# Linear attention with a channel mix on one core: the q transposes of batches 4 to 7 moved from TensorE to the DMA crossbar

## The chip, the cores and the metric

The kernel runs on one core of one Trainium2 chip. The metric is the device time of one execution in microseconds (us). Three timed runs of the kernel before gave 208.45, 209.91 and 210.52 us; the median, 209.91 us, is the time before. A core has five instruction streams that run beside each other: TensorE (PE; its weight loads are shown as PEld), VectorE (DVE), ScalarE (ACT), GpSimd (POOL) and SyncE (SP). Each works through its own list in order, and an instruction that waits for a semaphore holds back everything behind it in its list. Sixteen DMA engines move data for all of them.

## The reference

Two layers one after the other, for 8 batches, 8 heads, 576 positions and 64 numbers a head:

```
kv  = einsum('bhsd,bhse->bhde', k, v)
o   = einsum('bhsd,bhde->bhse', q, kv)
x   = o / sqrt(mean(o*o, axis=-1) + 1e-6) * g_norm        # to (batch, seq, 512)
xk  = mu_k * x + (1 - mu_k) * x_prev                      # x_prev: x one position earlier
xr  = mu_r * x + (1 - mu_r) * x_prev
out = sigmoid(xr @ w_r) * (relu(xk @ w_k)**2 @ w_v)       # w_k 512x1024, w_v 1024x512, w_r 512x512
```

## The kernel before

**Two stages.** `attention(b)` works on one batch, in two halves z of four heads each. `mix(g)` works on a group of 512 positions; there are nine groups, 0 to 8, and a group needs one or two batches (group 8 the last 512 positions, that is batch 7 alone).

**A plan of named pieces, one list.** `attention` and `mix` compute nothing at once: each `add(name, engines, function, ...)` registers a piece of work under a name. `ORDER`, a text of some 740 words at the head of the file, then says in which order the pieces are emitted, and a suffix `@A` or `@D` says whether a movable piece goes to ACT or to DVE. Since an engine works in order, `ORDER` sets the order on all five engines. The names, for batch b, half z, section i of the positions, group g:

- `ld.q b`, `ld.k b`, `ld.v b`: loads from HBM that turn float32 into bfloat16, issued by POOL (L251). Batches 0 and 1 are loaded by halves, the others whole. Each of k, v and q has three buffers.
- `q b.z` (L294): 36 TensorE transposes of 64x64 per half, into PSUM; `qc` copies the result to SBUF as `qT`.
- `kv b` (L286): k times v, 72 matmuls; `kc` copies the 128x256 result to SBUF.
- `u b.z i` (L301): q times kv, four matmuls for each section of 288 positions; `uc` copies to SBUF (`uT`), `sq` squares.
- `ss b`, `rs b`, `sp b.z`: the sum of squares of all heads (L409), the reciprocal root on ACT (L306, tile `rsc`, one buffer), and four DMAs per half, issued by SP, that spread it over the partitions (L455, tile `rs`). Batches 0 and 1 do without the spread.
- `mul`, `wr`, `d`, `mk`/`mr`, `xk`/`xr`: the normalised x and the two blends, on DVE and ACT (L423, L172/L174, L318, L178/L180, L331).
- `k g.f` (L542), `relu`, `ksq`; `r g.c` (L564), `sig`; `v g.c` (L584), `out`, `st`: the channel mix. `k`, `r` and `v` pieces are four matmuls of 512 columns with 128x128 weights. `out` multiplies on DVE, and `st` issues two DMAs to HBM (L493), on SP; only the last group also uses ACT for them.
- `z:512`: a matmul on zeros (L482), 34 of them, all in the first 20 us.

**PSUM** is split into four tiles of 128x2x512 float32. Two of them form a ring `at`, for everything in the attention, and two a ring `mm`, for the mix: a piece takes the next tile of its ring and waits until the reader of that tile's last content is done.

**SP's list** before is only `sp` and `st`: nothing in it waits for a load from HBM.

Of the kernel before, what the change touches and what calls it, by code (L numbers as in the profile page):

```python
# [25 lines left out]
mr0.1w@D mk0.1w@D ss1.0 xr0.0w ss1.1 ksq0.11 rs1.0 r0.3 xr0.1a rs1.1 q1.1 r0.0 qc1.1@D ld.k6.01 xr0.1w mul1.0 u1.11
sig0.1 u1.10 r0.1 uc1.11@D sq1.10@A v0.1.0 sq1.11@D sig0.0 xk0.1w ld.q4.01 uc1.10@D ss1.2 v0.1.1 wr1.0@D d1.0 ss1.3
v0.0.0 mk1.0@D rs1.2 xk1.0 v0.0.1 ld.v4.01 rs1.3 q2.0 mul1.1 q2.1 qc2.0@A v0.3.0 wr1.1@D d1.1 v0.3.1 out0.0 mk1.1@A
v0.2.0 st0.1 qc2.1@A xk1.1 v0.2.1 mr1.1@D k1.2 out0.1 k1.3 mr1.0@D kv2 relu1.1 k1.0 kc2@D ld.k4.01 xr1.0 ld.q5.01
u2.10 u2.01 uc2.10@D k1.1 uc2.01@A sq2.01@A sq2.10@D k1.6 relu1.0 u2.11 u2.00 uc2.11@A k1.7 uc2.00@D sq2.11@D k1.4  # L30
sq2.00@A xr1.1 relu1.3 k1.5 ksq1.3 ss2 kv3 ksq1.1 rs2 q3.0 ld.k5.01 sp2.0 r1.0 kc3@A relu1.2 qc3.0@D r1.1 ksq1.0
u3.01 q3.1 uc3.01@D sp2.1 r1.2 ld.q6.01 sq3.01@D ld.v5.01 r1.3 sig1.0 qc3.1@D ld.v6.01 ksq1.2 u3.00 u3.10 v1.0.0
uc3.00@D uc3.10@A st0.0 sq3.10@A sq3.00@D v1.0.1 sig1.1 mul2.0 u3.11 q4.1 wr2.0@D d2.0 v1.1.0 mk2.0@A v1.1.1 mul2.1
v1.3.0 qc4.1@A out1.0 v1.2.0 wr2.1@A xk2.0 uc3.11@A st1.0 v1.2.1 sq3.11@A d2.1 v1.3.1 st0.3 mk2.1@D xk2.1 ss3 kv4
out1.1 q4.0 k2.2 ld.q7.01 qc4.0@D rs3 ld.v7.01 k2.3 kc4@D sp3.0 mr2.1@D u4.11 u4.00 uc4.11@D k2.4 uc4.00@A relu2.1
sq4.11@D k2.5 sq4.00@D sp3.1 mr2.0@D u4.01 relu2.2 u4.10 uc4.01@D k2.0 sq4.10@A sq4.01@D k2.1 ksq2.1 uc4.10@A st1.1
xr2.0 ss4 relu2.0 q5.1 xr2.1 k2.6 ksq2.0 k2.7 mul3.0 qc5.1@D r2.0 relu2.3 r2.1 wr3.0@A ksq2.3 rs4 r2.2 ksq2.2 sp4.0
d3.0 r2.3 sig2.0 mk3.0@D q6.1 mul3.1 kv5 sig2.1 q5.0 qc6.1@D st1.3 v2.3.0 kc5@A qc5.0@D v2.1.0 st0.2 wr3.1@D d3.1
u5.11 u5.01 sp4.1 uc5.11@A v2.2.0 mk3.1@D uc5.01@A xk3.1 v2.3.1 mr3.1@D v2.2.1 sq5.01@D st1.2 sq5.11@D v2.0.0 xk3.0
out2.1 u5.10 kv6 uc5.10@A q6.0 ld.k7.01 mul4.0 v2.0.1 st2.2 qc6.0@A mr3.0@D v2.1.1 kc6@A sq5.10@D st2.3 xr3.1 k3.2  # L40
out2.0 u6.10 u5.00 k3.3 uc5.00@A mul4.1 st2.0 k3.4 xr3.0 relu3.1 wr4.1@D k3.5 d4.1 uc6.10@A r3.0 mr4.1@D relu3.2
sq5.00@D r3.1 sq6.10@D wr4.0@D ksq3.1 u6.01 sig3.0 ss5 uc6.01@D k3.0 d4.0 k3.1 sq6.01@D mk4.1@D rs5 kv7 mr4.0@D
relu3.0 q7.0 sp5.1 xr4.0 u6.00 k3.6 kc7@A ksq3.2 qc7.0@A k3.7 mk4.0@D ksq3.0 r3.2 relu3.3 sp5.0 uc6.00@D r3.3
sq6.00@D xk4.0 u6.11 q7.1 uc6.11@D v3.1.0 st2.1 ksq3.3 v3.0.0 sig3.1 mul5.1 v3.1.1 qc7.1@A sq6.11@D xk4.1 ss6 xr4.1
v3.0.1 r4.0 out3.0 r4.1 rs6 st3.0 u7.10 u7.11 sq7.10@A v3.2.0 uc7.11@A st3.1 uc7.10@D v3.3.0 sq7.11@D wr5.1@D sp6.0
u7.00 mul5.0 u7.01 v3.2.1 sig4.0 d5.1 v3.3.1 uc7.00@A wr5.0@A k4.6 sq7.00@A out3.1 sq7.01@A k4.7 uc7.01@A mk5.1@D
st3.2 ss7 d5.0 relu4.3 k4.2 sp6.1 mk5.0@D mr5.1@A k4.3 xk5.0 k4.4 ksq4.3 relu4.1 xr5.1 k4.5 xk5.1 k4.0 relu4.2
mul6.0 k4.1 mr5.0@D wr6.0@A d6.0 r4.2 relu4.0 r4.3 ksq4.0 k5.2 ksq4.1 sig4.1 mul6.1 k5.3 ksq4.2 v4.1.0 mr6.0@D rs7
xr5.0 v4.1.1 relu5.1 sp7.1 v4.0.0 wr6.1@A ksq5.1 v4.0.1 r5.0 out4.0 sp7.0 r5.1 mk6.0@D v4.3.0 d6.1 v4.2.0 mr6.1@D
# [25 lines left out]
class Plan:  # L75
# [8 lines left out]
    def emit(self, order, zeros):  # L84
        for word in order.split():
            if word.startswith("z:"):
                zeros(int(word[2:]))
                continue
            name, _, eng = word.partition("@")
            p = self.pieces[name]  # L90
            eng = eng or p.on
            assert len(eng) == 1 and eng in p.on and not p.done, word
            assert all(d.done for d in p.deps + p.also.get(eng, [])), word
            p.fn(eng)
            p.done = True
        assert all(p.done for p in self.pieces.values())
# [3 lines left out]
def kernel(  # L100
# [30 lines left out]
    CB = 2  # L131

# [9 lines left out]
        "kv": (2, (128, 2, NZ * HD), BF16),  # L142
# [11 lines left out]
        "mm": (2, (128, 2, 512), FP32),  # L154
        "at": (2, (128, 2, 512), FP32),
# [4 lines left out]
    def get(buf, dtype=None):  # L160
        if buf.t is None:
            n, shape, dt = BUFS[buf.tag]
            pool = psum if buf.tag in ("mm", "at") else sb
            buf.t = pool.tile(list(shape), dt, tag=buf.tag, name=buf.tag, bufs=n)
        return buf.t
# [73 lines left out]
    ps9 = Buf("at")  # L239
# [57 lines left out]
    def u_tiles(ps, kv, qT, z, c0, c1):  # L297
        for e in range(2):
            for y in range(2):
                rs_ = slice(64 * y, 64 * y + 64)  # L300
                nc.tensor.matmul(ps[64 * e:64 * e + 64, y, 0:c1 - c0], kv[rs_, e, HD * z:HD * z + HD],  # L301
                                 qT[rs_, e, c0:c1], start=True, stop=True)

# [40 lines left out]
    def section(b, z, i, name, qdep, kvc, kv, qT, uT, sq, rs):  # L344

        c0, c1 = PARTS[i] if b == 0 else (HS * i, HS * i + HS)
        w, cs = c1 - c0, slice(c0, c1)
        us = Buf("at")
        p_u = add("u" + name, "T", lambda _: u_tiles(get(us), kv.t, qT.t, z, c0, c1), deps=[qdep, kvc], bufs=[us, qT, kv])
# [12 lines left out]
    def attention(b):  # L362
# [7 lines left out]
        def kv_piece(name, ps, c, zs):  # L370
# [3 lines left out]
            return m, add("kc" + name, "DA", lambda eng: copy(eng, get(kv)[:, :, ks], ps.t[:, :, c + ks.start:c + ks.stop]),  # L374
                          deps=[m], bufs=[ps, kv])
# [9 lines left out]
        if b == 0:  # L385
            for z in range(NZ):
                _, kc = kv_piece(f"{b}.{z}", Buf("at"), 0, [z])
                kvcs.append(kc)
                for i, (c0, c1) in enumerate(PARTS):
                    qd[(z, i)] = q_piece(f"{b}.{z}{i}", z, Buf("at"), range(c0 // NP, c1 // NP), None)[1]  # L390
        else:
            ps0 = Buf("at")
            m, kc = kv_piece(f"{b}", ps0 if b > 2 else Buf("at"), KC, list(range(NZ)))
            kvcs = [kc, kc]
            for z in range(NZ):
# [257 lines left out]
```

## Time and profile before

| | |
|---|---|
| timed runs | 208.45, 209.91, 210.52 us |
| the profiled execution, its own time | 208.55 us |
| its span, first to last instruction | 206.6 us |
| VectorE, ScalarE, GpSimd busy | 137.8, 118.6, 26.4 us |
| bytes read from HBM / written | 33.56 MB / 9.44 MB |
| granted TensorE clock | 1.000 |

The span is 1.95 us shorter than the execution's own time; what lies around it is not in the profile. The costliest groups on TensorE and the groups that the change touches, in the profile's order of columns (line, engine, operation, output<-input, array tile, shape, count | busy us, mean ns of one | idle time ahead of them):

```profile
L584 PE MATMUL mm<-w_v,sqk 128*128 128x512 bf16 x272 | 62.6, 379 | 0.0
L542 PE MATMUL mm<-xk,w_k 128*128 128x512 bf16 x224 | 51.9, 379 | 0.0
L564 PE MATMUL mm<-w_r,xr 128*128 128x512 bf16 x144 | 34.1, 379 | 0.7 <-DVE w_r L180 0.7
L482 PE MATMUL mm<-zero 128*128 128x512 bf16 x34 | 10.9, 452 | 1.2 <-DVE zero L209 1.2
L294 PE MATMUL at<-ident,q 64*64 64x64 bf16 x576 | 8.0, 195 | 2.0 <-DMA q<-in_q_dram 1.2 <-ACT rs L306 0.4 <-POOL ident L224 0.4
L301 PE MATMUL at<-qT,kv 64*64 64x288 bf16 x112 | 6.7, 296 | 1.0 <-DVE qT L174 0.6 <-DVE kv L174 0.4
L286 PE MATMUL at<-v,k 64*64 64x64 bf16 x576 | 6.4, 194 | 3.4 <-ACT sig L574 1.4 <-DMA k<-in_k_dram 1.2 <-DMA v<-in_v_dram 0.7
```

The mean of one matmul is its time in the pipeline; matmuls overlap, so the time that a group takes of TensorE is its busy time. Busy time by stretches of ten us (columns: the stretch, its length, then the busy time and the count of instructions of PE, PEld, DVE, ACT and POOL, the granted clock, the DMA engines' busy share, GB/s):

```profile
20.00:30.00 10.00, 7.71 (x137) 6.39 (x138) 9.40 (x30) 8.38 (x16) 4.41 (x6) 1.00 1.22 206
50.00:60.00 10.00, 8.80 (x193) 4.30 (x192) 6.89 (x12) 6.40 (x9) 2.96 (x4) 1.00 1.20 217
80.00:90.00 10.00, 8.58 (x184) 4.30 (x183) 7.94 (x17) 5.63 (x8) 0.00 (x0) 1.00 1.19 240
100.00:110.00 10.00, 10.00 (x200) 4.85 (x196) 9.93 (x21) 9.74 (x11) 0.00 (x0) 1.00 0.35 83
150.00:160.00 10.00, 10.00 (x48) 4.56 (x47) 3.85 (x5) 3.91 (x4) 0.00 (x0) 1.00 0.23 52
```

A DMA share above 1 means that packets of several queues overlapped on an engine. It is at 1.2 while loads run and falls after 100 us.

### The profile page before, as it was taken

How to read it: one execution, taken by the hardware profiler on the slowest of the kernel's cores; microseconds unless marked ns; L12 is line 12 of the kernel's file. 1: busy time of each engine (PE TensorE's matmuls, PEld its weight loads, DVE VectorE, ACT ScalarE, POOL GpSimd, SP SyncE). 2: the span in 40 equal slices, each digit the busy share in tenths (PEclk: the TensorE clock that was granted, in tenths of full speed). 3: DMA queues.
4: the chain of work that ended last, by engine and by line, in shares of the span. 5: the costliest groups of instructions: out<-in, count | busy, mean ns of one | idle time of the engine just before them, and what ended most of it. 6: DMA issues, size and time to landing. Idle time of an engine off the chain costs nothing.

```text
span 206.6 us, 5133 instructions
## 1 busy us (share of the span) xinstructions
PE 193.2 (94%) x2172; PEld 95.7 (46%) x2172; DVE 137.8 (67%) x273; ACT 118.6 (57%) x151; POOL 26.4 (13%) x40
## 2 busy tenths in 40 slices
PE   7797979999799799799999999999999999999992
PEld 2344844544344444354443585444444444444441
DVE  1059988886585999698997798788733623421332
ACT  2279789867577395636896987716725032531310
POOL 7752532202140400000000000000000000000000
PEclk9999999999999999999999999999999999999999
DMA  4999999999999999999433650346004242604155
GB/s 75 162 207 205 206 208 205 208 216 221 210 238 236 231 252 242 223 264 268 116 91 77 149 122 0 71 94 156 0 0 102 62 93 61 143 0 102 24 133 153
DMA packets 25211, 30.10 MB, mean 146 GB/s; under 512 B 2524, under 2 KB 20708, under 8 KB 25188
## 3 DMA queue, kind: packets, MB, share of 16 engines
q0 software_dynamic: 15408, 16.78, 48.3%
q1 hardware_dynamic: 9380, 12.46, 24.0%
q10 hardware_dynamic: 400, 0.52, 0.7%
q8 instruction: 17, 0.28, 0.5%
q14 instruction: 6, 0.05, 0.1%
HBM read 33.56 MB, written 9.44 MB: 208 GB/s over the span
## 4 chain that ended last, share of the span: by engine, by line
PE 68%; DMA 20%; SPq 3%; ACT 2%; POOL 2%; issue 2%; DVE 1%; ACTq 0%; DVEq 0%; POOLq 0%
PE mm L584 26%; PE mm L542 24%; PE mm L564 12%; DMA w_r<-in_moe_w_r_dram 7%; DMA rs<-rsc 5%; DMA k<-in_k_dram 4%; DMA out_dram<-out 3%; SPq L455 2%; PE at L584 2%; PE at L301 2%; PE at L286 1%; PE at L294 1%; SPq L493 1%; POOL q L251 1%; ACT rsc L306 1%
## 5 line engine op out<-in xcount | busy, mean ns | idle before, releaser
L584 PE MATMUL mm<-w_v,sqk 128*128 128x512 bf16 x272 | 62.6, 379 | 0.0
L542 PE MATMUL mm<-xk,w_k 128*128 128x512 bf16 (+1 forms) x288 | 59.2, 356 | 0.0
L503 ACT ACTIVATE relu<-mm 128x1024 bf16<-128x1024 f32 x36 | 36.8, 1022 | 25.8 <-PE mm L542 23.4
L584 PEld LDWEIGHTS <-sqk 128*128 128x128 bf16 x296 | 28.2, 98 | 32.2 <-issue 1.4
L542 PEld LDWEIGHTS <-w_k 128*128 128x128 bf16 x288 | 27.2, 98 | 26.9 <-issue 1.6
L564 PE MATMUL mm<-w_r,xr 128*128 128x512 bf16 x144 | 34.1, 379 | 0.7 <-DVE w_r L180 0.7
L552 DVE TENSOR_TENSOR sqk<-relu 128x1024 bf16<-128x1024 bf16 x32 | 21.6, 687 | 16.4 <-ACT relu L503 16.4
L597 DVE TENSOR_TENSOR out<-mm,sig 128x1024 f32<-128x1024 f32 x16 | 19.6, 1222 | 18.6 <-PE mm L584 18.6
L574 ACT ACTIVATE sig<-mm 128x1024 bf16<-128x1024 f32 x18 | 18.3, 1024 | 22.5 <-PE mm L564 22.5
L564 PEld LDWEIGHTS <-xr 128*128 128x128 bf16 x144 | 13.7, 98 | 16.6 <-issue 1.0
L180 DVE TENSOR_SCALAR md<-d,cols 128x576 bf16<-128x576 bf16 (+2 forms) x62 | 18.2, 344 | 0.3
L172 ACT CAST uT<-at 128x576 bf16<-128x576 f32 (+1 forms) x18 | 11.4, 645 | 11.4 <-PE at L301 11.3
L423 DVE TENSOR_TENSOR xT<-uT,rs 128x1152 bf16<-128x1152 bf16 (+2 forms) x18 | 12.4, 686 | 4.8 <-DMA rs<-rsc 3.0
L188 ACT ACT_TABLE_LOAD x12 | 15.4, 1283 | 0.2
L174 DVE CAST uT<-at 128x576 bf16<-128x576 f32 (+1 forms) x14 | 10.4, 742 | 7.0 <-PE at L301 5.5
L318 DVE TENSOR_TENSOR d<-xT 128x1152 bf16<-128x1152 bf16 (+2 forms) x20 | 12.7, 634 | 0.8 <-ACT xT L172 0.5
L331 DVE TENSOR_TENSOR xk<-md,xT 128x1152 bf16<-128x1152 bf16 (+2 forms) x20 | 12.7, 633 | 0.6 <-ACT md L178 0.4
L331 DVE TENSOR_TENSOR xr<-md,xT 128x1152 bf16<-128x1152 bf16 (+2 forms) x20 | 12.5, 631 | 0.0
L482 PE MATMUL mm<-zero 128*128 128x512 bf16 x34 | 10.9, 452 | 1.2 <-DVE zero L209 1.2
L172 ACT COPY qT<-at 128x1152 bf16<-128x1152 bf16 (+2 forms) x8 | 8.0, 995 | 6.0 <-PE at L294 6.0
L178 ACT ACTIVATE md<-d,cols 128x256 bf16<-128x256 bf16 (+2 forms) x18 | 9.9, 600 | 1.8 <-DVE d L318 1.8
L174 DVE COPY qT<-at 128x1152 bf16<-128x1152 bf16 (+2 forms) x10 | 6.9, 693 | 4.7 <-ACT kv L172 4.2
(54 smaller groups left out, 139.3 us busy)
## 6 DMA issues: line engine op xcount, KB each, us to landing
out_dram<-out SPq DMA_DIRECT2D x67, 128.0 KB, 2.5
q<-in_q_dram POOLq DMA_DIRECT2D x6, 576.0 KB, 23.0
v<-in_v_dram POOLq DMA_DIRECT2D x6, 576.0 KB, 25.7
k<-in_k_dram POOLq DMA_DIRECT2D x6, 576.0 KB, 22.5
rs<-rsc SPq DMA_DIRECT2D x48, 72.0 KB, 5.0
q<-in_q_dram POOLq DMA_DIRECT2D x4, 288.0 KB, 9.7
k<-in_k_dram POOLq DMA_DIRECT2D x4, 288.0 KB, 11.4
v<-in_v_dram POOLq DMA_DIRECT2D x4, 288.0 KB, 11.0
```

Source lines behind the costliest of these rows:

```text
L172: nc.scalar.copy(out=dst, in_=src)
L174: nc.vector.tensor_copy(out=dst, in_=src)
L180: nc.vector.tensor_scalar(out=dst, in0=src, scalar1=col, scalar2=None, op0=ALU.mult)
L188: nc.scalar.preload_act_table_set(name)
L331: nc.vector.tensor_tensor(out=dst[:, 2 * z:2 * z + 2, r0:r0 + w], in0=md.t[:, :, cs], in1=xT[:, :, prev], op=ALU.add)
L503: nc.scalar.activation(out=get(rt), in_=ps.t, func=AF.Relu)
L542: nc.tensor.matmul(get(ps)[:, fc % 2, a0:a1], w_k_sb[:, cc, 128 * fc:128 * fc + 128], xk[:, cc, x0:x0 + a1 - a0], start=(cc == 0), stop=(c ...
L552: nc.vector.tensor_mul(out=get(sqk)[:, 2 * f2:2 * f2 + 2, :], in0=rt.t, in1=rt.t)
L564: nc.tensor.matmul(get(ps)[:, ci % 2, :], xr[:, cc, n0:n0 + 128], w_r_sb[:, cc, :], start=(cc == 0), stop=(cc == NHP - 1))
L574: nc.scalar.activation(out=get(sg), in_=ps.t, func=AF.Sigmoid)
L584: nc.tensor.matmul(get(ps)[:, bank, cs], sqk.t[:, fc, 128 * ci:128 * ci + 128], w_v_sb[:, fc, cs], start=(fc == 0), stop=(fc == NFC - 1))
L597: dv = add(f"out{g}.{c2}", "D", lambda _, ps=ps, sg=sg, ot=ot: nc.vector.tensor_mul(out=get(ot), in0=ps.t, in1=sg.t), deps=ms + [sg_done], ...
```

## The change

Four things change together.

1. **q of batches 4 to 7 (`XB = 4`) is transposed by DMA.** Instead of 36 TensorE transposes and a copy, a piece `xq b.z` issues one `dma_start_transpose` from SBUF to SBUF on SP's list. It turns the nine 128x128 blocks of a half (128x1152, bfloat16).
2. **kv is kept twice for these batches.** The DMA leaves each position block of q in the upper or the lower partition half, by the parity of the block. So kv is copied three times, once whole and once per half into the other half (`kc b.0`, `.1`, `.2`), `u_tiles_crossed` uses eight matmuls of 128 or 192 columns per section in place of four of 288, the sections have 320 and 256 positions, and `mul` is two instructions.
3. **PSUM tiles are free slots.** The two rings become four slots, and `ORDER` says with `#n` which slot a piece takes.
4. **`ORDER` is a new list** for all pieces, with other choices of ACT and DVE too, 35 zero matmuls, and the loads in another order: after the weights q2 v2 k2 v3 k3 q3 v4 k4 q4 v5 v7 q5 k5 k6 q7 q6 v6 k7.

The diff's core; of the new `ORDER` the parts around the new pieces:

```diff
+sq3.00@A u3.11#2 uc3.11@A sq3.11@A uc3.00@A st0.1 st0.0 v1.2.0#0 v1.3.0 v1.3.1 ld.q4.01 xq4.0 ld.v5.01 mul2.1
+wr2.1@D d2.1 mk2.1@D ss3#1 rs3 sp3.1 kv4#2 kc4.1@A kc4.2@A kc4.0@A mr2.1@A v1.2.1 v1.0.1 mul2.0 wr2.0@D d2.0 xk2.1
+mk2.0@D sp3.0 xq4.1 xk2.0 k2.4#1 k2.5 out1.0 st1.0 out1.1 st1.2 relu2.2 mr2.0@D ksq2.2 k2.2#3 k2.3 relu2.1 ld.v7.01
+ld.q5.01 st1.1 xq5.1 st1.3 ld.k5.01 u4.01#1 u4.00#0 sq4.00@A k2.0#2 k2.1 k2.6#3 k2.7 xr2.0 mul3.1 uc4.00@A relu2.0
+sq4.01@A relu2.3 xq5.0 xr2.1 r2.2#2 wr3.1@D d3.1 r2.3 sig2.1 r2.0#3 r2.1 sig2.0 ksq2.0 mul3.0 ksq2.1 v2.0.0#0 ksq2.3
+wr3.0@D uc4.01@D v2.1.0 ld.k6.01 ld.q7.01 ld.q6.01 xq6.0 ld.v6.01 d3.0 mk3.0@D xk3.0 u4.10#2 uc4.10@A u4.11#3
...
+xr3.1 st2.1 k3.1 relu3.0 ksq3.0 v2.2.0#3 ld.k7.01 ss4#0 rs4 sp4.0 sp4.1 u5.10#1 uc5.10@A u5.00#2 uc5.00@A sq5.00@A
...
+r3.2#1 u5.11#0 uc5.11@A xq7.0 xq7.1 sq5.11@A kv6#3 ksq3.3 kc6.1@D kc6.2@D u5.01#2 xq6.1 st2.0 st2.3 st2.2 r3.3
+uc5.01@A sq5.01@A sig3.1 v3.1.0#0 r3.0#2 r3.1 mul4.1 kc6.0@D mul4.0 ss5#3 v3.0.0 v3.1.1 v3.0.1 sig3.0 rs5 sp5.0
+v3.3.0#2 v3.2.0 wr4.0@D d4.0 mr4.0@A mk4.0@D wr4.1@D d4.1 mk4.1@D xk4.0 out3.0 sp5.1 st3.1 xk4.1 u6.01#3 uc6.01@D
+u6.11#1 uc6.11@D sq6.01@D sq6.11@D kv7#0 kc7.0@A kc7.1@A v3.3.1 kc7.2@D v3.2.1 out3.1 st3.3 u6.10#3 uc6.10@A
...
-        "kv": (2, (128, 2, NZ * HD), BF16),
+        "kv": (2, (128, 2, 2, NZ * HD), BF16),
...
-        "mm": (2, (128, 2, 512), FP32),
-        "at": (2, (128, 2, 512), FP32),
+        "ps": (4, (128, 2, 512), FP32),
...
+            if buf.tag == "ps":
+                buf.t = psum.tile(list(shape), dt, tag=f"ps{buf.slot}", name=f"ps{buf.slot}", bufs=1)
...
+    def u_tiles_crossed(ps, kv, qT, z, c0, c1):
+        blocks = qT.rearrange("p y c -> p (y c)").rearrange("p (m r) -> p m r", r=128)
+        j0, j1 = c0 // NP, c1 // NP
+        for odd in range(2):
+            js = [j for j in range(j0, j1) if j % 2 == odd]
+            for y in range(2):
+                half, m0, n = (NJ * y + js[0]) % 2, (NJ * y + js[0]) // 2, len(js)
+                rs_ = slice(64 * half, 64 * half + 64)
+                a = js[0] - j0
+                for e in range(2):
+                    o = ps[64 * e:64 * e + 64, half, 0:c1 - c0].rearrange("p (j c) -> p j c", c=NP)
+                    nc.tensor.matmul(o[:, a:a + 2 * n - 1:2, :], kv[rs_, half ^ y, e, HD * z:HD * z + HD],
+                                     blocks[rs_, m0:m0 + n, NP * e:NP * e + NP], start=True, stop=True)
...
+            copies = [((0, 128), 0, (0, 128))] + ([((64, 128), 1, (0, 64)), ((0, 64), 1, (64, 128))] if b >= XB else [])
...
+                def cross(_, z=z, qT=qT):
+                    nc.sync.dma_start_transpose(
+                        out=get(qT).rearrange("p y c -> p (y c)").rearrange("p (m r) -> p m r", r=128),
+                        in_=qin.t[:, 2 * z:2 * z + 2, :].rearrange("p y c -> p (y c)"))
+
+                x = add(f"xq{b}.{z}", "S", cross, deps=[loaded[("q", b, z)]], bufs=[qin, qT])
+                qd[(z, 0)] = qd[(z, 1)] = x
...
+                nc.vector.tensor_mul(out=o[:, :, 0::2, :], in0=x[:, :, 0::2, :], in1=y[:, :, 0::2, :])
+                nc.vector.tensor_mul(out=o[:, ::-1, 1::2, :], in0=x[:, :, 1::2, :], in1=y[:, :, 1::2, :])
```

SP's list after the change, by kind of DMA: `sp2` (8), `st0` (8), `xq4.0`, `sp3` (8), `xq4.1`, `st1` (6), `xq5.1`, `st1` (2), `xq5.0`, `xq6.0`, `st2.1` (2), `sp4` (8), `xq7.0`, `xq7.1`, `xq6.1`, `st2` (6), `sp5` (8), and then only `st` and `sp`.

## The prediction

> **What bounds the kernel now.** I read the page's shares first, then TensorE's waits, then its timeline to see how far each stage lags, then SP's list and the landings of single loads.
>
> ```profile
> span 206.6 us, 5133 instructions
> ...
> PE 193.2 (94%) x2172; PEld 95.7 (46%) x2172; DVE 137.8 (67%) x273; ACT 118.6 (57%) x151; POOL 26.4 (13%) x40
> ...
> PE   7797979999799799799999999999999999999992
> ...
> DMA  4999999999999999999433650346004242604155
> ...
> q0 software_dynamic: 15408, 16.78, 48.3%
> q1 hardware_dynamic: 9380, 12.46, 24.0%
> ```
>
> TensorE is the bound, but the span has two halves: up to 100 us the DMA engines are full and TensorE has gaps (the 7s), afterwards TensorE has none. So only TensorE work can shorten the second half, and the first half is a matter of what arrives when. TensorE's waits (total, times, longest):
>
> ```profile
> PE at L286 <- ACT sig L574: 1.4, 1, 1.4
> PE at L286 <- DMA k<-in_k_dram: 1.2, 2, 0.9
> PE at L294 <- DMA q<-in_q_dram: 1.2, 1, 1.2
> ...
> PE at L301 <- DVE kv L174: 0.4, 1, 0.4
> ```
>
> These lie at 54, 68, 72 and 84 us, as the timeline shows: 1.2 + 0.93 + 0.42 + 1.42 = 4.0 us.
>
> **The ledger.** The chain gives a price for each TensorE piece: 0.865 us for four 512-column matmuls (1.73 for eight), 0.72 for `kv`, 0.36 for 36 transposes, 0.18 for a `u`, 0.36 for `ss`, 0.32 for a zero (10.9/34). With the pieces of the old list (72 k, 36 r, 70 v and four half-size ones, 34 zeros and the attention) this sums to 188.7 us. TensorE's last matmul ends at 202.8 us by the chain, so 14.1 us are lost. Three starts show where:
>
> ```profile
> 45.12 0.78 PE L286 MATMUL at<-v,k 64*64 64x64 bf16 x72
> ...
> 52.06 0.43 PE L409 MATMUL at<-sq,heads 128*32 128x288 bf16 x8
> ...
> 69.48 1.90 PE L542 MATMUL mm<-xk,w_k 128*128 128x512 bf16 x8
> ...
> 84.16 0.77 PE L286 MATMUL at<-v,k 64*64 64x64 bf16 x72 [1.42 <-ACT sig L574]
> ```
>
> The list stands at 37.3, 44.0, 58.7 and 70.9 us there: 7.8, 8.1, 10.8 and 13.3 us lost; the rest is 0.8.
>
> **The change, part by part.**
>
> *TensorE work.* Eight pieces of 36 transposes go: 8 x 0.36 = 2.9 us. Sixteen `u` pieces have eight matmuls in place of four with the same columns in all. Each extra matmul costs between nothing and 46 ns (0.185 us for four in a pair of sections that took 0.37): 0 to 3.0 us. Nearest is the 64-column transpose, 0.36/36 = 10 ns, or 0.04 a section; weights of another half come in, so I take 0.06: 1.0 us. One more zero is 0.3. New sum 187.1: 1.6 us less.
>
> *VectorE and ScalarE.* Fewer `qc` (13 copies of 1152 become 6, 0.75 on DVE and 1.1 on ACT), eight more `kc` (about 0.4 each), `mul` in two (0.49 + 0.42 for 0.75), 12 `md` scalings moved to ACT: DVE loses some 10 us and ACT gains 12. Both end near 130 us, hidden by TensorE's 190: nothing, except where one of them is ahead of TensorE on a path (below); without that cover ACT's 12 us would count.
>
> *PSUM slots.* No instruction; they decide who waits for whom. Where it matters: `kv7` has slot 0, which `v3.0`/`v3.1` filled, so it waits for `out3.0`.
>
> *The crossbar pieces.* Each is 128x1152 bf16, 288 KB, as much as four spread DMAs. The trace has no transpose. DMA time at the least: the hardware queue's own rate, 24.0% of 206.6 us for 12.46 MB, is 4.0 us per MB, so 1.2 us. At the most: 256-byte pieces (one row of a block), 1152 of them, at that queue's mean per packet, 85 ns, over 16 engines: 6.1 us. I take 1.2, since rows of bytes are what the queue's price is made of. SP's time between one issue (5.42/8 = 0.68) and nine (6.1): I take 1.0. Landing 5 to 7 us after the issue while loads run, as the spreads (medians 5.0 to 7.0), 2.1 to 2.6 after.
>
> The Trainium skill weighs against the change: "VectorE: DVE Perf Modes", section "The three transpose paths", has 1309 ns for a 128x128 block by the DMA crossbar, 390 ns by TensorE, and says to use TensorE where a PSUM result will do. By it a piece of nine blocks one after another is, as an estimate, 11.8 us, and the sum would be that of the third rival. The trace agrees on the side but not on the size: TensorE takes 0.36 us here for such a piece, not nine times 390 ns, and of the crossbar no run shows anything yet.
>
> *What SP now waits for.* `xq` waits for a load, and SP's spreads and stores stand behind it. The loads are paced:
>
> ```profile
> 70.08 0.74 POOL L251 DMA_DIRECT2D q<-in_q_dram  x1 [10.27 <-PE at L294]
> ```
> ```profile
> q<-in_q_dram POOLq DMA_DIRECT2D x1, 576.0 KB, 22.2
> ```
>
> This is the 16th load after the weights: 92.3 us. Likewise the 3rd lands at 45.1, the 9th at 65.5, the 17th at 96.5. In the new list the 3rd is still k2, the 9th is q4, the 16th q6, the 17th v6. Up to q6 there are eight spreads fewer (0.29 us each by the queue's rate: -2.3), as many stores, and four crossbar pieces (+4.7): q6 at 94.7, v6 at 98.9.
>
> *POOL.* q6 takes q4's buffer, so its load waits for `xq4.1`, and v6 and k7 stand behind it. `xq4.1` follows `sp3` on SP and has landed by about 81, while k5, k6 and q7 are still in flight: nothing; each us after 92 would push q6 by one. `xq7.1` waits for the `qT` that `u5.11` frees, with `xq6.1`, `st2` and `sp5` behind it: `sp5` is due only after `ss5`, later than `u5.11`, so nothing there.
>
> **The walk.** Stage one stays as it is: `kv2` waits for the third load or for ACT and DVE, both near 45 to 47 us, and 7.7 us are lost when `ss2` ends, at 53.2.
>
> *Spread of batch 2.* Before:
>
> ```profile
> 53.31 5.42 SPq L455 DMA_DIRECT2D rs<-rsc  x8
> ```
> ```profile
> 64.92 0.76 DVE L423 TENSOR_TENSOR xT<-uT,rs 128x1152 bf16<-128x1152 bf16 x1 [2.04 <-DMA rs<-rsc]
> ```
>
> From the end of `rs2` (53.3) to the second `mul` 11.6 us pass. Now `rs2` ends at 54.0, so the second `mul` is at 65.6, and `k2.4` needs 3.9 us of DVE more (mul, wr, d, xk, two md, xk): 69.5. TensorE is there at 58.3 + 7.7 = 66.0 and waits 3.5. Lost 11.2. The four old waits are avoided: k4 is now the 8th load (61.4) for a `kv4` at 63.5.
>
> *q4.* SP has `xq4.0` out at 66.5, landed at 72 to 73.5, and `u4.01` is due at 72.9: 0.3. `sp3.1` follows by 70.2, lands 6.8 later at 77, and `mul3.1` and `xr2.1` end at 78.5; `r2.2` is due at 77.2: 1.3. Lost 12.7 or so. `kv6` at 98.9 then finds v6 just landed.
>
> *q6.* SP cannot issue `st2.1` and `sp4` before q6 has landed: 94.7, +1.0 (`xq6.0`), +1.2 (two stores), +5.4 (eight spreads) = 102.3, landed by 106 (2.6 to 5.0 later). Behind `mul4.1` DVE has, up to `out3.0`: mul 0.9, kc 0.4, mul 0.9, wr 0.2, d 0.75, md 0.74, wr 0.2, d 0.75, md 0.74, xk 0.75, out 1.22, that is 7.5 us: 113.6. `kv7` is due at 95.8 + 12.7 = 108.5 and waits 5.1. Lost 17.8, and 0.8 as before in the rest: 18.6.
>
> TensorE ends at 187.1 + 18.6 = 205.7. Behind it come 3.8 us in the span (206.6 - 202.8; the last two pieces are the same) and 1.95 around it: 211.4. The profiled execution before took 208.55, 1.36 under the median of the runs, which I add: **212.8 us**. A difference of 1% (2 us) is about what a measurement of this kernel can tell.
>
> **Rivals.** *First, faster:* SP's block costs nothing, since `mul4.1` starts in time for `kv7`. It decides at q6's landing: below 89 us (108.5 less 7.5, 2.6 to 5 and 7.6) there is no wait, and TensorE loses 13.5 us. Then 187.1 + 13.5 + 5.75 + 1.36 = 207.7, and 205.7 if the first stage loses only what the third load forces (39.4 listed at 45.1: 5.7, not 7.7): about 206.5. For it: the 5 to 7 us come from a queue that stores fill as well, and SP has no other stores then. Against: fifteen loads at 2.85 us (k3 lands at 51.5, q3 at 54.3) are ahead anyway. Chance 0.28.
>
> *Second, even:* the two new waits together cost what 1.6 us of work and 4.0 us of old waits give, as when spreads land 2.5 us sooner at both places. About 210. Chance 0.18.
>
> *Third, small pieces:* 6.1 us of DMA time each. `xq4.0` lands at 78 (+5 at `u4`), q6 20 us later, and `kv7` with it: +22 on the forecast's 212.8 less what the first wait hides, about 230. Against it, the spreads' rows of 1152 bytes go at the queue's rate. Chance 0.10.
>
> That the change does not do what it says is excluded by the instruction lists: eight transposes on SP, 288 matmuls fewer.
>
> **The numbers.** The forecast has 0.44; its own range is 210.5 (q6 at 92) to 216 (xq at twice its price), 0.06 of it within 1%. Faster 0.28; same 0.18 + 0.06 = 0.24; slower 0.38 + 0.10 = 0.48. From 205.5 to 217 leaves out the third rival and the lower end of the first.
>
> **What would show it.** TensorE's waits should have `k2` waiting for DVE near 66 us and `kv7` for `out3.0` near 108; SP's list a transpose that waits for q6 until about 95; 288 transposes on TensorE; the DMA share full until 102 to 105. Wrong it would be if q6 landed before 89 us, or if transposes took DMA time unlike the spreads'.

## The result, and the profile after

| | before | after |
|---|---|---|
| time, median of 4 runs each | 210.22 us (208.45 to 210.84) | 225.62 us (224.17 to 226.31) |
| ratio, with its 95% interval | | 1.0757 (1.0711 to 1.0804) |
| profiled execution: its own time, span | 208.55 us, 206.6 us | 224.17 us, 221.9 us |
| mean TensorE clock granted | 1.00 | 0.949 |

The change makes the kernel 7.6% slower. The side was forecast; the size was not: 225.6 us against 212.8, and above the upper end of the range, 217. Below, the ratios to the kernel before are compared, since that kernel was timed again beside each group of experiments (its medians were 209.6 to 210.2 us). A median counts every execution of a kernel, a ratio only those within 1.5% of its shortest.

The page of the changed kernel:

```profile
span 221.9 us, 4725 instructions
...
PE 196.3 (88%) x1949; PEld 95.2 (43%) x1949; DVE 129.4 (58%) x260; ACT 127.9 (58%) x171; POOL 26.2 (12%) x40
...
PE   7899979999887289931999999999999999999991
...
PEclk9999999999997859995599999999999999999998
...
q1 hardware_dynamic: 18852, 14.82, 29.9%
```

Read the third line against that of before: the small gaps of the first half (the 7s) are mostly gone, and two wide holes stand in their place, near 75 us (the 2) and 100 us (the 3 and the 1). In the clock row, which had only 9s before, the 7, 8, 5 and 5, 5 follow on these holes. The hardware queue has twice as many packets as before (18,852 for 9,380) for a fifth more bytes. TensorE's waits name what ends the holes:

```profile
PE ps L329 <- DMA qT<-q: 13.6, 2, 8.4
PE ps L590 <- DVE xk L359: 2.3, 1, 2.3
```

and its timeline says where (start, duration, line, tiles, then the idle time before and what ended it):

```profile
68.19 5.31 PE L590 MATMUL ps<-xk,w_k 128*128 128x512 bf16 x16 [2.30 <-DVE xk L359]
78.74 0.69 PE L329 MATMUL ps<-qT,kv 64*64 64x128 bf16 x16 [5.23 <-DMA qT<-q]
...
89.94 0.44 PE L329 MATMUL ps<-qT,kv 64*64 64x192 bf16 x16
...
104.58 0.48 PE L329 MATMUL ps<-qT,kv 64*64 64x192 bf16 x8 [8.38 <-DMA qT<-q]
```

These are `k2.4`, `u4.01` with `u4.00`, `u4.10` with `u4.11`, and `u5.00`. Two of the crossbar's pieces are late for their readers, by 5.2 and 8.4 us. SP's list has their issues:

```profile
64.82 1.79 SPq L431 DMA_TRANSPOSE qT<-q  x1
66.72 12.44 SPq L503 DMA_DIRECT2D rs<-rsc  x8
79.31 2.21 SPq L431 DMA_TRANSPOSE qT<-q  x1
...
90.56 9.62 SPq L431 DMA_TRANSPOSE qT<-q  x2
...
101.93 5.59 SPq L503 DMA_DIRECT2D rs<-rsc  x8
```

`xq4.0` is issued at 64.82 and its reader starts at 78.74; `xq5.0` is issued at 90.56 (the row of two holds `xq6.0` as well, which waits until 97.40 for q6) and its reader starts at 104.58: 14 us each from issue to landing. The eight spreads of batch 3, which follow the first one, take 12.4 us to leave where the spreads of batch 2 took 5.4 before. Seven of them leave by 71.8; the eighth is issued at 78.62, as soon as the transpose has landed. Leaving early does not help the seven: of the 512 packets of the eight spreads none starts before 77.5 us, when the piece's own packets are nearly through. They stand behind the piece in the hardware queue that SP fills (q1 of the page).

The trace of single packets shows what is slow about the landing. Every crossbar piece is 1152 packets of 256 bytes; the table has, for each, its first and last packet and how many load packets (1152 bytes each) started in between.

```
piece   first packet  last packet  time us   load packets
xq4.0       69.01        78.04       9.0        1211
xq4.1       83.42        88.84       5.4         517
xq5.1       90.58        91.83       1.3           0
xq5.0       94.61       102.92       8.3        1164
xq6.0      102.93       105.21       2.3          28
xq7.0      108.82       110.35       1.5           0
xq7.1      117.93       119.43       1.5           0
xq6.1      119.43       120.95       1.5           0
```

Beside a full load queue, one load packet passes for each packet of the piece (1211 and 1164 for 1152). A load packet took 106 ns (median), so 1211 of them on 16 engines are 8.0 of the 9.0 us. The Trainium skill has this rule in "DMA: Bandwidth & Descriptors", section "Queues, rings and completion order": each engine goes round between the queue rows that have work, packet by packet. The counts agree with it. Alone, a piece needs 1.3 to 1.5 us here. The packets are not all of the 14 us: 4.2 us pass between the issue of `xq4.0` and its first packet, while the queue still moves the stores that were issued ahead of it, and 4.1 us for `xq5.0`, for which nothing here shows a reason.

Last, the clock. The windows of the trace give TensorE's busy time, the granted clock (after POOL's count), the DMA share and the rate for each stretch:

```profile
68.20:73.50 5.30, 5.30 (x16) 1.90 (x16) 4.12 (x6) 1.02 (x1) 0.00 (x0) 0.68 1.24 201
73.50:78.70 5.20, 0.01 (x1) 0.00 (x0) 0.00 (x0) 1.02 (x1) 0.00 (x0) 0.77 1.22 203
78.70:85.00 6.30, 6.26 (x34) 2.66 (x35) 3.05 (x6) 2.93 (x5) 0.00 (x0) 0.65 1.21 225
...
104.60:110.00 5.40, 5.40 (x20) 1.96 (x21) 0.00 (x0) 1.30 (x2) 0.00 (x0) 0.50 0.89 221
110.00:116.00 6.00, 6.00 (x28) 2.70 (x27) 1.92 (x2) 2.41 (x3) 0.00 (x0) 0.96 0.05 9
```

After each of the three standstills TensorE works on at a lower clock. The values are means: the clock record of the trace has 0.50 from 69.5 to 72.9, from 76.3 to 83.1 and from 100.2 to 110.4 us, and 1.00 in between. In the four busy stretches that is (1 - 0.68) x 5.3 + (1 - 0.65) x 6.3 + (1 - 0.50) x 5.4 + (1 - 0.96) x 6.0 = 1.7 + 2.2 + 2.7 + 0.2 = 6.8 us of matmul time. "TensorE: Matmul & The Clock Gate", Part 1, of the Trainium skill has the clock fall to half after an idle window of about 3.4 us; here a standstill of 2.3 us was followed by it too. The runs give no threshold: in the experiments below a standstill of 1.9 us was followed by half the clock (before 104.9 us, in the first kernel of "Towards a faster kernel"), and one of 2.0 us was not (before 67.4 us, in "Is it the loads?").

The sum closes. With the ledger of the forecast for the listed TensorE work, 187.1 us, the 9.9 us lost when `k2.4` starts (68.2 less the 58.3 listed ahead of it), the waits of 5.2 and 8.4 and the clock's 6.8, TensorE ends at 217.4, which is where its last matmul ends in the trace. The tail behind it is 4.5 us, for 3.8 before.

### The profile page after: what moved, and what is told of

It is laid out like the page before. It is cut to its first block, busy times and chain, and to the rows that moved or that the text cites. A ratio compares the mean times of both kernels' runs of the same rounds, so it can differ in the third digit from the quotient of the medians.

```text
span 221.9 us, 4725 instructions
## 1 busy us (share of the span) xinstructions
PE 196.3 (88%) x1949; PEld 95.2 (43%) x1949; DVE 129.4 (58%) x260; ACT 127.9 (58%) x171; POOL 26.2 (12%) x40
## 3 DMA queue, kind: packets, MB, share of 16 engines
q1 hardware_dynamic: 18852, 14.82, 29.9%
## 4 chain that ended last, share of the span: by engine, by line
PE 70%; DMA 24%; POOL 2%; issue 1%; DVE 0%; POOLq 0%
PE ps L632 28%; PE ps L590 24%; PE ps L612 13%; DMA qT<-q 13%; DMA w_v<-in_moe_w_v_dram 6%; DMA w_k<-in_moe_w_k_dram 6%; PE ps L298 2%; PE ps L329 2%; PE ps L451 1%; POOL q L263 1%; PE ps L313 1%; PE ps L306 1%; POOL k L263 1%; POOL v L263 1%; PE ps L512 0%
## 5 line engine op out<-in xcount | busy, mean ns | idle before, releaser
L632 PE MATMUL ps<-w_v,sqk 128*128 128x512 bf16 (+1 forms) x296 | 70.2, 384 | 0.9 <-issue 0.6
L590 PE MATMUL ps<-xk,w_k 128*128 128x512 bf16 (+1 forms) x288 | 63.0, 371 | 2.3 <-DVE xk L359 2.3
L551 ACT ACTIVATE relu<-ps 128x1024 bf16<-128x1024 f32 x36 | 36.4, 1024 | 34.7 <-PE ps L590 34.6
L612 PE MATMUL ps<-w_r,xr 128*128 128x512 bf16 x144 | 34.5, 379 | 0.0
L645 DVE TENSOR_TENSOR out<-ps,sig 128x1024 f32<-128x1024 f32 x16 | 19.4, 1221 | 21.6 <-PE ps L632 21.5
L622 ACT ACTIVATE sig<-ps 128x1024 bf16<-128x1024 f32 x18 | 18.1, 1024 | 18.9 <-PE ps L612 12.5
L184 ACT CAST uT<-ps 128x640 bf16<-128x640 f32 (+2 forms) x22 | 14.1, 646 | 10.3 <-PE ps L329 9.4
L190 ACT ACTIVATE md<-d,cols 128x576 bf16<-128x576 bf16 (+2 forms) x30 | 18.1, 657 | 1.8 <-DVE d L346 1.8
L329 PE MATMUL ps<-qT,kv 64*64 64x128 bf16 (+1 forms) x128 | 4.3, 247 | 13.6 <-DMA qT<-q 13.6
L384 ACT ACTIVATE sq<-ps 128x640 bf16<-128x640 f32 (+2 forms) x17 | 11.2, 660 | 7.2 <-PE ps L329 4.9
L530 PE MATMUL ps<-zero 128*128 128x512 bf16 x35 | 10.6, 439 | 1.2 <-DVE zero L221 1.2
```

The costliest lines, as they stand in the source:

```text
L184: nc.scalar.copy(out=dst, in_=src)
L190: nc.scalar.mul(out=dst, in_=src, mul=col)
L551: nc.scalar.activation(out=get(rt), in_=ps.t, func=AF.Relu)
L590: nc.tensor.matmul(get(ps)[:, fc % 2, a0:a1], w_k_sb[:, cc, 128 * fc:128 * fc + 128], xk[:, cc, x0:x0 + a1 - a0], start=(cc == 0), stop=(c ...
L612: nc.tensor.matmul(get(ps)[:, ci % 2, :], xr[:, cc, n0:n0 + 128], w_r_sb[:, cc, :], start=(cc == 0), stop=(cc == NHP - 1))
L622: nc.scalar.activation(out=get(sg), in_=ps.t, func=AF.Sigmoid)
```

## The experiments

Two theories stood against each other. Mine: the late landing beside the loads is the cause, through the readers of batches 4 and 5, and with the crossbar out of the loads' way the new list is faster than the old one. The rival: what the pieces do to SP's list and to the DMA engines costs as much without any reader, or the new order is worse by itself.

**Which part of the change costs.** First the new list with no crossbar at all. Its q pieces had to be put into the list by me, and the last two `kc` of a batch go.

```diff
-    XB = 4
+    XB = 8
...
-xq4.0 xq4.1 xq5.1 xq5.0 xq6.0 xq7.0 xq7.1 xq6.1
+q4.0#2 qc4.0@D q4.1#2 qc4.1@A q5.1#0 q5.0#1 qc5.1@D qc5.0@D q6.0#1 q6.1#3 qc6.0@A qc6.1@D q7.0#1 qc7.0@A q7.1#0 qc7.1@A
```

> The new list, the new slots and the new loads' order alone: q of all batches by TensorE again, no crossbar piece, no second copy of kv. Late landing (the eight crossbar pieces take 12 to 14 us to land, so u4 and u5 wait 5.2 + 8.4 us and TensorE then runs 6.8 us longer at half clock): these 20.4 us go and 2.9 - 1.0 us of TensorE work comes back, 225.6 - 20.4 + 1.9 = about 207 us. Rival, the new list itself is worse: 215 us or more, with other waits of TensorE in place of those on qT.

It took 220.09 us, ratio 1.0530 (1.0462 to 1.0598): the rival's number. Its largest wait:

```profile
115.37 1.18 PE L297 MATMUL ps<-v,k 64*64 64x64 bf16 x72 [3.63 <-DVE out L644]
```

That is `kv7`, waiting for `out3.0`: the wait that I had forecast for the changed kernel, and which isn't found there. It is 3.6 us of some 10.5 lost; the rest was not traced to single waits. But this run does not convict the list, as the next one shows; my places for q6 and q7 in lists that are full at that point may be the cost, and that was not separated.

The crossbar for batches 6 and 7 alone, with the same places for q4 and q5:

```diff
-    XB = 4
+    XB = 6
```

> The crossbar for batches 6 and 7 only, q of 4 and 5 by TensorE. Late landing: no wait at u4 and u5, their crossbar pieces of 6 and 7 fall after the loads and land in under 4 us: 225.6 - 20.4 + 1 = about 206 us. Rival of the record (SP's list is held by xq6.0 until q6 has landed, so the spread of batch 4 is late and kv7 waits some 5 us for out3.0): 211 us, with that wait in TensorE's list.

210.61 us, ratio 1.0035 (0.9997 to 1.0073): the same as before. It is the rival's number, but without the rival's wait: `kv7` doesn't wait for `out3.0` here. The spreads of batch 3 leave SP in 5.8 us, and no wait for `qT<-q` is left. So the new list, its slots and the crossbar for batches 6 and 7 together neither gain nor lose; the 7% are those of batches 4 and 5.

**Without readers.** The kernel above, with the four pieces of batches 4 and 5 at their places in the list, into tiles that nothing reads (their q goes by TensorE as well):

```diff
+                spare = const.tile([128, 2, S], BF16, name=f"spare{b}{z}")
...
+                    nc.sync.dma_start_transpose(out=spare..., in_=qin...)
```

> As the one before, and the four crossbar pieces of batches 4 and 5 are issued too, at their old places, into tiles that nobody reads: their time on SP and on the DMA engines without a reader. Late landing: what cost time was that u4 and u5 wait for them, so within 3 us of the one before, about 207 to 209 us. Rival, SP's list and the DMA engines' time are the cost: 214 us or more, with waits on the spreads of batches 3 and 4.

220.32 us, ratio 1.0527 (1.0450 to 1.0604). My theory fell: 4.9% of the 7.2% between 1.0035 and 1.0757 are lost without a reader. The SP list and the timelines of VectorE and TensorE say how:

```profile
65.28 1.73 SPq L441 DMA_TRANSPOSE spare<-q  x1
67.12 13.42 SPq L512 DMA_DIRECT2D rs<-rsc  x8
```
```profile
82.43 0.76 DVE L476 TENSOR_TENSOR xT<-uT,rs 128x1152 bf16<-128x1152 bf16 x1 [7.10 <-DMA rs<-rsc]
```
```profile
83.92 4.45 PE L621 MATMUL ps<-w_r,xr 128*128 128x512 bf16 x10 [4.77 <-DVE xr L359]
```

VectorE stands 7.1 us at `mul3.1` with `xr2.1` behind it in its list, and the r pieces of group 2 wait 4.8 us. `mul3.1` needs only the first four spreads of batch 3, `sp3.1`. They leave SP by 70.4 us, but all the packets of the eight spreads run from 79.0 us on, behind those of the piece (69.5 to 79.3). So it is the queue behind SP that holds them. On SP itself only the eighth spread is held, until 80.0 us, and `mul3.0`, which needs it, starts at 85.3 without a wait.

**SP's list.** The same kernel with `xq4.0` moved behind the spreads of batch 3:

```diff
-xq4.0 ... sp3.1 ... sp3.0 xq4.1
+sp3.1 ... sp3.0 xq4.0 xq4.1
```

> The kernel with spare crossbar pieces (batches 4 and 5 by TensorE, four crossbar pieces into tiles that nobody reads; 220.3 us), with the first spare piece moved on SP behind the spreads of batch 3. Theory (a spare piece ahead of the spreads costs through SP: only eight DMAs of its list can be open, so the last spread waits until the piece lands): the eight spreads leave in 6 us (13.4 before), the wait of the r pieces of group 2 for xr (4.8 us) shrinks to under 1, time 214 to 217. Rival (the pieces cost DMA time and delay spreads and loads wherever they stand): the wait keeps 3 us or more, time 219 or more.

216.64 us, ratio 1.0337 (1.0287 to 1.0388), 1.9% or 4 us under the last. The spreads leave at once, their packets run from 70.2 to 76.7 us, and the wait at 84 us is gone:

```profile
66.12 5.81 SPq L512 DMA_DIRECT2D rs<-rsc  x8
72.07 10.56 SPq L441 DMA_TRANSPOSE spare<-q  x2
```
```profile
111.91 0.43 PE L460 MATMUL ps<-sq,heads 128*32 128x288 bf16 x8 [3.07 <-DVE kv L186]
```

So the place on SP's list, which is the place in the queue behind it, is a price of its own. What is left shows 30 us on, where VectorE again stands at a `mul`, now that of batch 4. I took it for the load of q6, which starts at 89.4 us only, when the piece that reads its buffer has landed.

**POOL's hold.** Two kernels read a weight tile in place of q, so that q6's load need not wait for a piece: the first with the pieces at their old places, the second with the first piece behind the spreads.

```diff
-                        in_=qin.t[:, 2 * z:2 * z + 2, :].rearrange("p y c -> p (y c)"))
+                        in_=w_v_sb.rearrange("p a c -> p (a c)")[:, 0:2 * S])
```

> The kernel with spare crossbar pieces, at their old places, but they read a weight tile and not q, so that q6's load doesn't wait for a spare piece to land. Theory (a part of the price is that POOL holds q6's load, and v6 and k7 behind it, until the piece of batch 4 has landed): q6's load starts by 84 us (90.3 with the hold, 83.3 without pieces), its transposes and the spreads of batch 4 leave 4 to 6 us earlier, time 215 to 218. Rival (the loads are late anyway, from the DMA time of the pieces): within 1% of 220.3.

220.80 us, but from 217.04 to 223.09, ratio 1.0436 (1.0327 to 1.0545; of two executions): not to be told from the 1.0527 with the hold. Nor did the edit do what it was for: q6's load started at 88.5, now held by TensorE's own q4 pieces, which come late.

> The kernel with spare crossbar pieces, the first of them behind the spreads of batch 3 (216.6 us so far), and now reading a weight tile and not q, so that q6's load need not wait for a spare piece. Theory (what is left of the price there is the held load: q6 late, so the transpose of q6 holds SP, the spreads of batch 4 are late, VectorE's list stands at mul4, and TensorE waits 3.1 us for VectorE near 112 us): q6's load starts by 85 us, the spreads of batch 4 leave before 98, the wait near 112 us goes, time 211.5 to 214. Rival (the pieces' own DMA time delays loads and spreads): the wait stays above 2 us, time 215.5 to 217.5.

221.15 us, ratio 1.0519 (1.0472 to 1.0567), 1.8% above the kernel with the hold, so this theory fell as well, and on its own ground: q6's load did start early, at 82.5 us. Its profile, which is of the longest of its five executions (226.65 us), has these lines:

```profile
86.08 10.08 SPq L441 DMA_TRANSPOSE spare<-w_v  x1
96.20 1.90 SPq L550 DMA_DIRECT2D out_dram<-out  x2
98.14 5.64 SPq L441 DMA_TRANSPOSE spare<-w_v  x1
```

The third and fourth piece now run beside the loads that came sooner. With the hold, the third one found no load in flight and went through in 2.5 us; here its packets run from 97.0 to 105.6 us with 737 load packets between them. Loads and pieces share the engines packet by packet, and here starting the one sooner made the other late. That this is also what costs the four executions between 218.95 and 221.28 us is not shown: none of them has a trace. So the 7.2% of batches 4 and 5 come apart as follows: 2.3% go with the readers, 1.9% with the place of the first piece, and the 3.0% that are left (1.0337 less 1.0035) stay open. The DMA time of the pieces themselves is the rival that no run rules out.

**Is it the loads?** The changed kernel, in which POOL reads one element of `xq4.0`'s result before it starts v5's load and the others:

```diff
-ld.q4.01 xq4.0 ld.v5.01
+ld.q4.01 xq4.0 hold ld.v5.01
...
+                    add("hold", "P", lambda _, qT=qT: nc.gpsimd.tensor_copy(out=tiny, in_=qT.t[0:1, 0, 0:1]))
```

> The changed kernel, with one added wait: GpSimd reads one element of the transposed q of batch 4 (half 0) before it starts v5's load and all loads behind it. So the first crossbar piece runs with no load in flight. Theory (the piece's 256-byte packets take turns with load packets, and this is what makes its landing late): it lands 5 to 7 us after its issue instead of 14, so near 71 us; u4.01 no longer waits for it (5.2 us before), the eight spreads of batch 3 leave SP in 6 us instead of 12.4. The loads start 6 us later in exchange, so the time itself falls little: 219 to 225. Rival (a crossbar piece needs 13 to 14 us by itself in the first half of the kernel): landing still at 78 or later, u4.01 waits as before or longer, time 226 or more.

227.49 us, ratio 1.0848 (1.0785 to 1.0911). POOL's and SP's lists:

```profile
67.50 0.18 POOL L436 COPY tiny<-qT 1x1 bf16<-1x1 bf16 x1 [27.74 <-DMA qT<-q]
```
```profile
64.14 1.40 SPq L430 DMA_TRANSPOSE qT<-q  x1
65.65 5.32 SPq L505 DMA_DIRECT2D rs<-rsc  x8
```

The piece that took 14 us lands 3.4 us after its issue (64.14 to 67.50), its packets between 65.43 and 66.95 with no load packet among them; the spreads behind it leave in 5.3 us for 12.4, and `u4.01` starts at 70.95 without a wait. That the loads make the piece land late is shown. The time did not come out as I had put it (219 to 225): the next three pieces meet the held loads (1224, 1155 and 871 load packets among theirs), and TensorE waits for `qT` 5.2, 2.9 and 9.0 us later on.

**The clock.** The changed kernel with matmuls on zeros ahead of the three pieces that wait, into PSUM tiles that the pieces overwrite:

```diff
+    WARM = {"u4.01": 24, "u5.00": 38, "k2.4": 10}
+    def warm(name, ps):
+        for _ in range(WARM.get(name, 0)):
+            nc.tensor.matmul(get(ps)[:, 0, :], zero[:, 0:128], zero, start=True, stop=True)
```

> The changed kernel with zero matmuls ahead of k2.4 (10), u4.01 (24) and u5.00 (38), as many as their waits hold at 0.216 us each; nothing that is computed changes. If the half clock of 69 to 73, 76 to 83 and 100 to 110 us follows from TensorE standing still, it stays at 1.0 and the 6.8 us go: about 219 us, with the waits on qT as they are. If the clock falls for another reason, or the waits alone are the cost: 225 us.

222.72 us, ratio 1.0658 (1.0601 to 1.0714). The clock stays up all the way (mean 0.997):

```profile
PEclk9999999999999999999999999999999999999998
```

That the standstill lowers the clock is shown. It gives back about 1% (2 to 3 us) of the 6.8: a TensorE that is sooner at `u4.10` waits there for `xq4.1`, 1.7 us, where the slow clock had covered it.

**The old list.** The order, loads and PSUM rings of before, with the crossbar for 6 and 7, its first pieces ahead of the spreads of batch 4:

```diff
-... sp4.0 ...
+... xq6.1 xq6.0 sp4.0 ... xq7.0 xq7.1 st2.2 ...
```

> The list, loads and PSUM rings of before, with the crossbar for batches 6 and 7 alone: q6 ahead of the spreads of batch 4 on SP, q7 behind them. Theory: four pieces of 36 transposes leave TensorE (1.44 us) and the pieces land before their readers (u6 at 95, u7 at 113 us before), as loads end near 97 us: 208 to 209.5. Rival (q6's pieces run beside the last loads and hold the spreads of batch 4 on SP, as in the changed kernel): 212 or more, with TensorE waiting for qT or for xk of batch 4.

220.52 us, ratio 1.0524 (1.0473 to 1.0575). Two pieces ahead of the spreads of batch 4 cost the old list as much as the four without readers cost the new one:

```profile
80.68 10.58 SPq L430 DMA_TRANSPOSE qT<-q  x2
91.35 2.53 SPq L502 DMA_DIRECT2D rs<-rsc  x4
93.93 7.45 SPq L540 DMA_DIRECT2D out_dram<-out  x4
101.47 2.52 SPq L502 DMA_DIRECT2D rs<-rsc  x4
```

Two pieces among loads hold SP for 10.6 us, and their last packet comes at 100.3. The first half of the spreads, issued from 91.4 on, has its first packet at 99.4 and reaches VectorE's `mul` at 102.3 only, after 9 us of idle time there; the second leaves at 101.5, for 86.9 before. TensorE waits 7.3 us for a `kv` copy that stands behind that `mul`. And with batch 7 alone, whose pieces meet no load (their packets took 2.0 and 1.6 us):

```diff
-... sp5.1 sp5.0 ...
+... xq7.1 sp5.1 sp5.0 xq7.0 ...
```

> The list, loads and PSUM rings of before, with the crossbar for batch 7 alone, its two pieces around the spreads of batch 5, behind the last load. Theory (a crossbar piece that runs beside no load and stands in front of no late spread costs nothing, and saves TensorE two pieces of 36 transposes, 0.72 us): 208.7 to 209.5, half a per cent or less under before. Rival (two copies of kv more, and the smaller u pieces, take as much as they give): 209.8 to 211.

210.36 us, ratio 1.0032 (1.0005 to 1.0059): no gain. A piece that collides with nothing costs little, but the 0.72 us of TensorE work that it saves is not seen either.

**Towards a faster kernel.** From the kernel with the crossbar for 6 and 7: q of batches 4 and 5 put where TensorE or ScalarE stood, and eight matmuls on zeros ahead of `k2.4`.

```diff
-k2.4#1 q4.0#2 k2.5
+q4.0#2 qc4.0@A k2.4#1 k2.5 q4.1#2
...
-k3.0#2 sq4.11@D
+q5.0#1 k3.0#2 sq4.11@D qc5.0@A
...
```

> The crossbar for batches 6 and 7 alone (210.6 us so far), with q of batches 4 and 5 put where TensorE or ScalarE had nothing to do: q4.0 ahead of k2.4 and q4.1 behind k2.5, their copies on ScalarE; q5.0 ahead of k3.0; and eight matmuls on zeros ahead of k2.4, where TensorE stands for 2.9 us and the clock then falls. Theory (the waits of 0.8, 0.9, 0.4 and 1.0 us for qT and for PSUM between 75 and 92 us come from where I had put these pieces, the clock from the standstill): 206.5 to 208.5, below before. Rival (the first wait, for the spreads of batch 2, sets the pace, and other waits come in place of these): 209.5 to 211.

210.50 us, ratio 1.0015 (0.9986 to 1.0045): the rival's number. The old waits are gone, but a new one came:

```profile
104.88 0.43 PE L456 MATMUL ps<-sq,heads 128*32 128x288 bf16 x8 [1.86 <-DVE kv L185]
```
```profile
92.22 1.36 SPq L436 DMA_TRANSPOSE qT<-q  x1
93.68 1.28 SPq L546 DMA_DIRECT2D out_dram<-out  x2
95.05 6.92 SPq L508 DMA_DIRECT2D rs<-rsc  x8
```

`rs4` ends at 90.7, but SP stands at `xq6.0` until q6 has landed, and the spreads leave at 95.1. This is the mechanism that I had forecast, in its place. So one word was moved:

```diff
-xq6.0 ... sp4.0 sp4.1
+sp4.0 sp4.1 xq6.0
```

> The kernel with the crossbar for batches 6 and 7 and the four q pieces put elsewhere (210.5 us so far), with one word moved: q6's first crossbar piece behind the spreads of batch 4 on SP. There rs4 ends at 90.7 us, but SP stands until 92.2 for q6 to land and the spreads leave at 95.1; VectorE then stands 2.75 us at mul4 and TensorE 1.86 us for VectorE at 104.9. Theory (a transpose that waits for its load holds the spreads behind it): the spreads leave by 92 us, TensorE's wait near 105 us goes, 207.8 to 209.3, under before. Rival (the piece of q6 comes too late for u6, or another wait takes the place): 210 to 212.

The wait at 105 us went, and the spreads left at 90.98, but the six executions lie on two levels: 206.9 and 207.1, and four between 210.2 and 210.9 (median 210.26 us; the ratio, 0.9874 with the interval 0.9825 to 0.9924, rests on the two short ones). The trace, of one at 210.3, has another wait:

```profile
118.11 4.15 PE L596 MATMUL ps<-xk,w_k 128*128 128x256 bf16 x23 [2.48 <-ACT rsc L333]
```
```profile
117.32 0.74 ACT L333 ACTIVATE rsc<-ps,eps 128x576 bf16<-128x576 f32 x1 [3.02 <-DMA rs<-rsc]
```

`rs6` can't write `rsc` until the spreads of batch 5 have read it, and the PSUM slot that `rs6` reads is the one that `k4.0` needs. There is one `rsc` buffer; a second one:

```diff
-        "rsc": (1, (128, S), BF16),
+        "rsc": (2, (128, S), BF16),
```

> The kernel before this one (crossbar for batches 6 and 7, q6's first piece behind the spreads of batch 4), with two rsc buffers in place of one, so that rs6 need not wait until the spreads of batch 5 have landed. Theory (the executions at 210.3 us are those in which TensorE waits 2.5 us behind rs6 at 118 us; without collisions the smaller TensorE work is paid out): that wait is gone, 206.5 to 208 in nearly all executions, 1% under before. Rival (the upper level has another cause, or another wait comes in): two levels stay, the median at 209.5 or more.

208.39 us (206.57 to 209.42, 12 runs), ratio 0.9948 (0.9916 to 0.9981): half a per cent under the kernel before, the first that beats it, and the wait at 118 us is gone. It is less than I expected, and how much of it a second `rsc` buffer would give the old kernel was not tried.

## Why the prediction was wrong

**The step that failed: "Landing 5 to 7 us after the issue while loads run, as the spreads".** It was 13.9 and 14.0 us for the two pieces that met full loads, and 3.4 us without loads. I had priced a piece by its bytes, as the spreads; beside loads its packets took 9.0 and 8.3 us, by their count, one load packet for each. (The eight spreads of a batch are 512 packets of 1152 bytes.) The other 5 to 6 us, most of them ahead of the first packet, are explained for `xq4.0` alone, by the stores in the queue. From this step `u4.01` waited 5.2 us in place of 0.3, and `u5.00`, of which the walk says nothing, 8.4. These waits are not all that the pieces cost: without any reader 4.9% of the 7.2% stay.

**"DMA time at the least 1.2 us ... I take 1.2" was right as far as it goes:** 1.3 to 1.5 alone. The third rival had the size of the packets right, 256 bytes, and even the landing ("`xq4.0` lands at 78 (+5 at `u4`)"), but by another reason, 6.1 us of work for 16 engines, at 85 ns a packet; a packet of a piece took 18 ns alone and 31 ns beside loads (medians). So the landing was luck. Its consequence, q6 20 us later, did not come (q6 landed at 97.4, forecast 94.7). The estimate of 11.8 us that I had made from the page "VectorE: DVE Perf Modes", section "The three transpose paths", of the Trainium skill is not what nine blocks take here either: 1.5 us alone, 8 to 9 beside loads.

**SP.** "SP's time ... I take 1.0" is mis-sized (1.3 to 2.9 us for one transpose). The larger miss is what stands behind: I let SP wait for a piece's load only, and had `sp3.1` land 6.8 us after it left. The packets of `sp3` stood in the queue behind those of `xq4.0` until 77.5 us, so the late landing reached `mul3.1` (81.3 us, forecast: done with `xr2.1` at 78.5); but the wait of `r2.2` that this brings, 4.8 us where nothing else is late, was covered in the changed kernel by `u4.01`'s own.

**"SP cannot issue `st2.1` and `sp4` before q6 has landed" was right**: SP stands until 97.4 us for q6, and the spreads of batch 4 leave from 101.9 to 107.5 (forecast: done at 102.3). But `kv7` did not wait: TensorE came to it at 126 us, not at 108.5, after 13.6 us of waits that I did not have. The wait came with some lists only: 3.6 us in the list without crossbar; none with the crossbar for batches 6 and 7, where TensorE was at `kv7` at 112.5 us; and in another place 1.9 us, which one moved word removed.

**"`xq4.1` ... has landed by about 81 ...: nothing"** failed too: q6's load started at 89.9 us. Yet its price of nothing was not refuted: of the kernels without readers, the one whose q6 load starts sooner is no faster. That is luck, as I had not argued it.

**Terms that held.** The wait of `k2.4` was 2.3 us for 3.5, `r2.2`'s 0 for 1.3. The ledger holds: from `k2.4` on it lists 128.8 us, and TensorE is busy for 135.6 us there, 6.8 of them the clock's. Two `u` pieces with eight matmuls each take 0.44 us, as the pairs with four before, so of the 1.0 us for these little shows. The clock was not in the sum at all and took 6.8 us. The tail behind TensorE's last matmul was 4.5 us for 3.8. Two counts of the working are off, without weight in the sum: 14 copies of 1152 become 6, not 13, and the matmuls fall by 223 (2172 to 1949), as 64 more of `u` and one on zeros stand against the 288 transposes.

In terms of the walk: 9.9 lost in place of 11.2 at `k2.4`; then 5.2, 8.4 and 6.8 (`u4.01`, `u5.00`, the clock) in place of 0.3, 1.3 and 5.1 (`u4.01`, `r2.2`, `kv7`) and 0.8 for the rest; 30.3 us in place of 18.6.

## What to carry to other kernels

Price a transfer that shares the engines with a full queue by the number of its packets, and not by its bytes: 288 KB in 1152 packets took 8 to 9 us beside loads and 1.5 us alone. Before a slow transfer is put on a queue, look at what stands behind it there and who waits for that, since a transfer that has left its engine's list can still stand in the queue: without any reader, four such pieces cost 5%, and two of the five went when one of them stood behind the spreads and not ahead. When two kinds of transfers compete, starting one sooner moves the delay to the other; only what runs after the last load was close to free.

## What the runs showed of the hardware that I had not expected

- Crossbar packets and load packets alternate one for one: 1211 and 1164 load packets beside 1152 of a piece, 517 and 28 where the loads ran dry.
- In SP's hardware queue the packets of later DMAs ran behind those of an earlier one: the spreads that left from 66.7 us on, behind `xq4.0`, have their first packet at 77.5, and the last packet of `xq4.0` starts at 78.0.
- Behind a DMA that has not landed, seven more of SP's list left, and the eighth waited: 71.8 to 78.6 us in the changed kernel; 5.3 us for all eight where the piece landed in 3.4. In the trace the eighth waits for the semaphore that the transpose raises (115), so this is a matter of the program's semaphores.
- A transpose took SP 1.3 to 2.9 us to issue in the changed kernel, a spread about 0.6. Right behind another piece that was still among loads it took 8.2 us (on the old list, at 83.05 us) and 10.1 us (the row at 86.08 us under "POOL's hold").
- Around standstills of 2.3, 5.2 and 8.4 us TensorE's clock was at half for 3.4, 6.8 and 10.2 us (69.5 to 72.9, 76.3 to 83.1, 100.2 to 110.4); with matmuls on zeros in these places it did not fall (mean 0.997).
